# First two tiles of a fused convolution and two-layer kernel: taps on VectorE in PSUM, tap pairs on TensorE, Exp on ScalarE, narrower first weights

## The chip, the cores and the metric

One NeuronCore of a Trainium2 chip runs the kernel. The metric is the device time of one execution in microseconds (us). The five engines are TensorE (PE, matrix products), VectorE (DVE), ScalarE (ACT), GpSimd (POOL) and SyncE (SP, which here only issues transfers). Each works through its own queue in order and waits for the others at semaphores.

## What is computed

The input is x, 2 sequences of 4096 positions with 192 channels, and 8 heads of 7 taps. The taps of a head go through a softmax, each channel is convolved causally with its head's 7 taps, and two dense stages follow on the 8192 tokens:

```python
w = np.exp(weight - weight.max(-1, keepdims=True))
w = w / (w.sum(-1, keepdims=True) + 1e-09)
out = np.einsum('hk,bskhg->bshg', w, x_unf)          # 7 taps, causal
x = out.reshape(8192, 192)
x = (sigmoid(x @ w_gate) * (x @ w_val)) @ w_out       # 192 -> 1536 -> 192
h = x @ w_in                                          # 192 -> 2048
P = a[0] + a[1]*h + a[2]*h**2 + a[3]*h**3
Q = 1 + abs(b[0])*abs(h) + abs(b[1])*h**2
out = (P / (Q + 1e-6)) @ w_out2                       # 2048 -> 192
```

Weights come to the device as 64-bit floats.

## The kernel before

Channels lie on partitions: 128 in a first block, the other 64 (R) in a second. Tokens are cut into 16 tiles of 512. Every operand of a product is split into a high and a low part (fp32r), so that a 192-channel product takes five matmuls: `mm128` (lines 1027 to 1029: high weight by high x, low weight by high x, high weight by low x) and `mm64` (lines 1035 and 1036), in which the 64 channels of the second block lie twice, on the lower and the upper 64 partitions, so that high and low weights go in one matmul.

For each tile `conv` convolves, `moe1` runs pass A (gate and val, 12 blocks of 128 columns, 10 matmuls a block) and pass B (5 matmuls a block), and `moe2` runs pass C (16 blocks, 5 matmuls each) and pass D (5 matmuls each; in the last tile, 12 blocks take two full fp32 matmuls instead). That is 340 matmuls a tile.

Weights are loaded once, in pieces of columns. `to_f32` (line 794) takes a piece through a transfer, one rounding and one Prelu activation on ScalarE (lines 807 and 711) and one bit operation on VectorE (line 816); `split_rows` and `split_tail` then make the high part (a copy, mostly on ScalarE) and the low part (a subtraction, line 722). Gate and val columns come in pieces of 256, 256, 512 and 512 (`cw1`). A piece of `w_gate` rows, of `w_val` rows and of the 64 remaining rows of both must be split before the blocks of pass A which it covers can run. There are 12 buffers of kind `f` (4 KB a partition) through which raw pieces, split pieces and later values pass.

The softmax of the taps (`small`, line 739) makes exp from two sigmoids, since Sigmoid's table is needed next anyway, and normalises the taps on VectorE before anything uses them. Tile 0: the first 128 channels are convolved by VectorE, one instruction a tap, in SBUF (`conv_vector`, lines 952 and 954); the second block, for tiles 0 and 1 together, is convolved by TensorE with 7 full fp32 products against diagonal matrices of the taps (`conv_first`, line 943), which GpSimd builds (line 936). Tile 1's first block and everything from tile 2 on are convolved by GpSimd, two instructions a tap (`conv_taps`, lines 920 and 923). `warm_up` runs 18 bf16 matmuls on zeros (line 965) before.

The order of all instructions is written out by hand: `PROGRAM` lists the 4747 operations of the plan by number, with a letter where another engine than the first choice takes one; buffers of a kind are given out by a planner (`Plan.order`), which runs at build time. An operation on GpSimd that shares VectorE's port is held behind an earlier VectorE operation of that sort (the `gate` at the end of the kernel). Transfers go out from SP's queue, the four first pieces of weights from ScalarE's.

Of the kernel before, what the change touches and what calls it, by code (L numbers as in the profile page):

```python
# [90 lines left out]
class Plan:  # L91
# [50 lines left out]
    def free_slots(self, kind, sort):  # L142

        got, held = [], 0
        for i, b in enumerate(self.slots[kind]):
            if b is None:
                got.append((0.0, i))
                continue
            if b.freed is None and all(u.end is not None for u in b.users):
                b.freed = max(u.end + FREE[u.eng] for u in b.users)  # L150
            if b.freed is not None:
                got.append((b.freed, i))
            elif b.sort == sort:
                held += 1
        return [] if held >= self.caps.get(sort, 1000) else sorted(got)

    def fit(self, o):

        t, places, used = 0.0, [], set()
        for b in o.bufs:  # L160
            if b.slot is not None:
                continue
            for s, i in self.free_slots(b.kind, b.sort):
                if (b.kind, i) not in used:
                    used.add((b.kind, i))
                    places.append((b, i))
                    t = max(t, s)
                    break
            else:
                return None, None  # L170
        return t, places

    def order(self, look, switch):


        free = dict.fromkeys(ENGINES, 0.0)
        avail = {e: [] for e in ENGINES}
        table, lock_free, clock = "sig", 0.0, Clock()

        def add(o):  # L180
            for e in o.opts:
                avail[e].append(o)

        def begin(o, e):
            t = max(free[e], o.ready, lock_free if o.opts[e][2] else 0.0)
            for b in o.bufs:
                for d, end in b.last.items():
                    if d != e:
                        t = max(t, end + HOP[d][e])
            return t  # L190

        for o in self.ops:
            if o.left == 0:
                add(o)
        for _ in self.ops:
            best = None
            for eng in ENGINES:
                found = []
                for i, o in enumerate(avail[eng]):
                    start = begin(o, eng)  # L200
                    if len(o.opts) > 1:
                        ends = {e: begin(o, e) + v[0] + v[3] for e, v in o.opts.items()}
                        if ends[eng] > min(ends.values()):
                            continue
                    found.append((start, o.prio + (switch if o.table and o.table != table else 0.0), i, o,
                                  max(free[eng], o.ready)))
                found.sort(key=lambda e: e[:3])
                pick, first = None, None
                for start, prio, _, o, asked in found:
                    if first is not None and start > first + look[eng]:  # L210
                        break
                    t, places = self.fit(o)
                    if t is None:
                        continue
                    start = max(start, t)
                    if first is None or start < first:
                        first = start
                    key = (max(0.0, start - first - look[eng]), prio)
                    if pick is None or key < pick[0] or pick[1] > first + look[eng]:
                        pick = (key, start, max(asked, t), o, places, eng)  # L220
                if pick is not None and (best is None or pick[1:3] < best[0:2]):
                    best = pick[1:]
            assert best is not None, "no operation can go on"
            o, places, eng = best[2:]
            o.eng, o.start = eng, best[0]
            cost, o.emit, lock, _ = o.opts[eng]
            frees = FREES[eng] if lock is True else lock
            if o.table and table != o.table:
                cost += TABLE
                table = o.table  # L230
            if eng == "PE" and o.start > free[eng] + 1.0:
                cost += STALL / FAST
# [352 lines left out]
    warm=18,  # L585
# [30 lines left out]
def conv_gated_rational_kernel(  # L616
# [639 lines left out]
    if warm:  # L1256
        warm_up(warm)
# [65 lines left out]
```

## Time and profile before

| | |
|---|---|
| median of 3 runs (lowest to highest) | 1278.5 us (1278.0 to 1279.02) |
| the profiled execution, its own time | 1277.71 us |
| span of its trace, first to last instruction | 1275.9 us |
| mean granted TensorE clock | 0.996 |
| PE, DVE, ACT, POOL busy, share of the span | 99%, 87%, 86%, 56% |

The profile shows one execution. Busy times of an engine are of instructions in flight: a matmul of 512 columns is shown with 389 ns, while the next one starts some 227 ns after it, so a busy share of TensorE close to 100% says that matmuls follow one another, and their number in a stretch says how fast. What the engines do at the start of the kernel is read from stretches and from the list of instructions in order of time, since the page's totals are those of 16 tiles.

### The profile page before, as it was taken

To read this page: it belongs to the slowest core of one execution; us is meant where nothing else is said; L and a number is where in the kernel's file an instruction comes from. 1 tells how busy PE (TensorE), PEld (TensorE's weight loads), DVE (VectorE), ACT (ScalarE), POOL (GpSimd) and SP (SyncE) were. 2 spreads that over 40 slices of the span, in tenths; PEclk is the share of its full clock that TensorE was granted. 3 is DMA by queue.
4 is the path that set the end of the run, shared out by engine and by line. 5 is a ranking of instruction groups with operands and counts; after the bars stand their busy time and mean duration, and the time that the engine had idled before them with its cause. 6 is when DMAs were issued, how large, how long until landed. Compare 5 with 4: busy or idle time off the path is not lost.

```text
span 1275.9 us, 15239 instructions
## 1 busy us (share of the span) xinstructions
PE 1260.0 (99%) x5460; PEld 1021.4 (80%) x5460; DVE 1114.8 (87%) x1362; ACT 1094.7 (86%) x1408; POOL 708.6 (56%) x466
## 2 busy tenths in 40 slices
PE   7999999999999999999999999999999999999998
PEld 3778888888888888888888888888888888888884
DVE  6989899989889888789888988878898887889996
ACT  7988988888887989887897897889888897789996
POOL 4476656665655575763565664866454745464530
PEclk9999999999999999999999999999999999999999
DMA  7621000010000100001010010100001000000000
GB/s 200 194 79 26 1 17 13 1 38 1 5 25 1 38 1 18 13 1 38 1 29 1 9 30 1 29 1 27 12 1 29 9 22 1 1 21 1 13 13 12
DMA packets 16716, 31.01 MB, mean 24 GB/s; under 512 B 2560, under 2 KB 6272, under 8 KB 16640
## 3 DMA queue, kind: packets, MB, share of 16 engines
q1 hardware_dynamic: 16192, 29.26, 8.2%
q8 instruction: 42, 0.69, 0.2%
q10 hardware_dynamic: 448, 0.79, 0.2%
q14 instruction: 34, 0.28, 0.1%
HBM read 19.81 MB, written 6.29 MB: 20 GB/s over the span
## 4 chain that ended last, share of the span: by engine, by line
PE 92%; DVE 4%; ACT 2%; issue 1%; DMA 1%; POOL 0%; SPq 0%; DVEq 0%; ACTq 0%; POOLq 0%
PE w L1027 11%; PE w L1035 11%; PE w L1036 11%; PE w L1028 11%; PE w L1029 11%; PE accd L1052 4%; PE accd L1061 4%; PE accd L1054 4%; PE accd L1062 4%; PE accd L1053 4%; PE accb L1052 3%; PE accb L1054 3%; PE accb L1053 3%; PE accb L1061 3%; PE accb L1062 3%; ACT f L711 1%
## 5 line engine op out<-in xcount | busy, mean ns | idle before, releaser
L711 ACT ACTIVATE f<-w,av 128x512 f32<-128x512 f32 x256 | 196.2, 778 | 49.5 <-PE w L1036 45.9
L720 POOL TENSOR_TENSOR r<-f,r 128x1024 fp32r<-128x1024 f32 x66 | 178.2, 2704 | 86.9 <-DVE f L1191 13.3
L1191 DVE TENSOR_TENSOR f<-f,w 128x512 f32<-128x512 f32 x256 | 172.4, 681 | 42.7 <-ACT f L711 41.9
L711 ACT ACTIVATE f<-w,kv 128x512 f32<-128x512 f32 x256 | 171.1, 686 | 41.4 <-PE w L1036 34.0
L722 DVE TENSOR_TENSOR r<-f,r 128x1024 fp32r<-128x1024 f32 x152 | 194.3, 1285 | 9.9 <-ACT r L711 4.4
L706 POOL TENSOR_SCALAR r<-f 128x1024 fp32r<-128x1024 f32 x77 | 114.1, 1483 | 139.1 <-DVE f L1216 28.1
L1193 DVE SCALAR_TENSOR_TENSOR f<-f,av,w 128x512 f32<-128x512 f32 x256 | 186.6, 743 | 4.8 <-ACT f L711 1.0
L923 POOL TENSOR_TENSOR ca<-ca,tmp 128x512 f32<-128x512 f32 x90 | 148.6, 1652 | 68.2 <-DVE f L1216 18.5
L1216 DVE SCALAR_TENSOR_TENSOR f<-f,av,f 128x1024 f32<-128x1024 f32 x128 | 171.7, 1347 | 9.4 <-ACT f L711 9.3
L1197 DVE SCALAR_TENSOR_TENSOR f<-f,bv 128x1024 f32<-128x1024 f32 x128 | 168.1, 1319 | 10.4 <-ACT f L711 10.2
L711 ACT ACT_TABLE_LOAD x130 | 166.8, 1283 | 5.0 <-DVE f L1197 1.5
L1097 DVE TENSOR_TENSOR f<-f,w 128x512 f32<-128x512 f32 x192 | 130.4, 681 | 46.2 <-PE w L1036 26.6
L920 POOL TENSOR_SCALAR tmp<-xa,cw 128x512 f32<-128x512 f32 x90 | 103.5, 1150 | 107.2 <-DVE f L1216 25.6
L711 ACT ACTIVATE f<-f,kv 128x1024 f32<-128x1024 f32 x128 | 156.4, 1241 | 1.2 <-DVE f L1197 0.3
L711 ACT ACTIVATE f<-f 128x1024 f32<-128x1024 f32 (+3 forms) x160 | 151.8, 960 | 0.8 <-DVE wo_s L870 0.2
L711 ACT ACTIVATE f<-w 128x512 f32<-128x512 f32 x192 | 113.2, 594 | 35.7 <-PE w L1036 32.6
L711 ACT ACTIVATE r<-f 128x1024 fp32r<-128x1024 f32 x99 | 103.8, 1056 | 10.4 <-DVE f L1097 4.7
L1027 PE MATMUL w<-yha,w_h 128*128 128x512 f32 x256 | 100.1, 391 | 0.2
L1029 PE MATMUL w<-yla,w_h 128*128 128x512 f32 x256 | 99.7, 389 | 0.0
L1028 PE MATMUL w<-yha,w_l 128*128 128x512 f32 x256 | 99.7, 389 | 0.0
L1036 PE MATMUL w<-ylb,w_b 128*128 128x512 f32 x256 | 99.6, 389 | 0.0
L1035 PE MATMUL w<-yhb,w_b 128*128 128x512 f32 x256 | 99.6, 389 | 0.0
(152 smaller groups left out, 3095.7 us busy)
## 6 DMA issues: line engine op xcount, KB each, us to landing
f<-in_wo SPq DMA_DIRECT2D x14, 384.0 KB, 3.7
xa<-in_xt SPq DMA_DIRECT2D x16, 259.0 KB, 3.2
out_dram<-f SPq DMA_DIRECT2D x16, 256.0 KB, 2.6
xb<-in_xt SPq DMA_DIRECT2D x16, 129.5 KB, 2.9
f<-in_w SPq DMA_DIRECT2D x4, 512.0 KB, 4.3
out_dram<-f SPq DMA_DIRECT2D x16, 128.0 KB, 2.4
xhb<-xhb SPq DMA_DIRECT2D x15, 128.0 KB, 2.3
xlb<-xlb SPq DMA_DIRECT2D x15, 128.0 KB, 2.2
```

Of the source, the lines that this page charges most:

```text
L711: plan.op("ACT", (53 if psum else 95) + n * 0.832 + 93 * ptr + own, prio, lambda: nc.scalar.activation(out=out(), in_=in_(), func=func, ** ...
L720: alts.append(("POOL", 147 + n * 2.105, lambda: nc.gpsimd.tensor_tensor(out=out(), in0=in0(), in1=f(in1()), op=ALU.subtract), True, H[alt] ...
L722: dve(prio, n, lambda: nc.vector.tensor_tensor(out=out(), in0=in0(), in1=f(in1()), op=ALU.subtract), rd, wr, lock=lock, alts=alts)
L1027: nc.tensor.matmul(o, lhsT=wh.tile[:, c], rhs=ha, start=True, stop=False)
L1028: nc.tensor.matmul(o, lhsT=wl.tile[:, c], rhs=ha, start=False, stop=False)
L1029: nc.tensor.matmul(o, lhsT=wh.tile[:, c], rhs=la, start=False, stop=False)
L1035: nc.tensor.matmul(o, lhsT=wb.tile[:, c], rhs=hb, start=False, stop=False)
L1036: nc.tensor.matmul(o, lhsT=wb.tile[:, c], rhs=lb, start=False, stop=True)
L1191: dve(at("v", t, p), sn, lambda q=q, cut=cut, h=h: nc.vector.tensor_tensor(out=cut(u[q]), in0=cut(u[q]), in1=h(), op=ALU.mult), [ps_, (u[q ...
L1193: dve(at("w", t, p), sn, lambda q=q, cut=cut, h=h: nc.vector.scalar_tensor_tensor(out=cut(u[q]), in0=cut(u[q]), scalar=av.tile[:, 1:2], in ...
L1197: dve(at("y", t, p), gn, lambda q=q: nc.vector.scalar_tensor_tensor(out=C(ha[q]), in0=C(ha[q]), scalar=bv.tile[:, 0:1], in1=C(ha[q]), op0= ...
L1216: dve(at("g", t, p), gn, lambda k=k: nc.vector.scalar_tensor_tensor(out=C(u[k]), in0=C(u[k]), scalar=av.tile[:, 0:1], in1=C(ha[k]), op0=AL ...
```

## The change

The order text is another one (4777 operations), and a second text, `SLOTS`, gives each buffer its place; the planner's `order`, `fit`, `free_slots` and `Clock` go. In it:

- `small` takes exp with ScalarE's Exp, then at once a Sigmoid on one element. Taps are used unnormalised (`cwe`); the sum and its reciprocal are made beside, and the reciprocal comes in as the scale of the operations that split the convolved tile (`xs`). The normalised taps for the later tiles are one GpSimd operation.
- For tiles 0 and 1 VectorE convolves the first block, now with the running sum in PSUM (`conv_vector`; bank `accd1`). TensorE convolves the second block with two taps per product: the 64 channels lie twice on the partitions, the second copy one token later (`load_pair`), and 4 products a tile take taps 0 and 1, 2 and 3, 4 and 5, and 6 (`pair_weights`, `conv_pairs`). Their output has both copies that `mm64` wants. Tile 1 is so no longer convolved on GpSimd.
- The first weights are 128, 128, 256, 512 and 512 columns wide; all of them come over SP's queue, and ScalarE's queue loads `xa` of tile 0.
- 12 matmuls on zeros instead of 18; their zeros are written by VectorE.
- Which engine takes a copy or a subtraction is now the order text's choice alone. Of the 218 copies that make high parts of `moe1` and `moe2` values it puts 99 on ScalarE, 75 on GpSimd and 44 on VectorE; of the 20 low parts of gate and val weights 12 on GpSimd and 8 on VectorE.

```diff
-        plan.op("DVE", 350, START, sm, rd=[cw], wr=[cw, wsum])
-        def ex():
-            nc.scalar.activation(out=ng, in_=w, func=ACTF.Sigmoid, scale=-1.0)
-            nc.scalar.activation(out=w, in_=w, func=ACTF.Sigmoid)
...
+        plan.op("DVE", 400, START, sm, rd=[cw, z], wr=[cw, wsum])
+        plan.op("ACT", 230, START, lambda: nc.scalar.activation(out=cwe.tile, in_=w, func=ACTF.Exp), rd=[cw], wr=[cwe])
+        plan.op("ACT", 200 + 1283, START, lambda: nc.scalar.activation(
+            out=first.tile, in_=cwe.tile[:, 0, 0:1], func=ACTF.Sigmoid), rd=[cwe], wr=[first])
+        for r0, k0, m in ((0, 0, 4), (R, 1, 3)):
...
+            plan.op("ACT", 200, START + 1, pick_act, rd=[cwe], wr=[(cwp, r0)],
+                    alts=[("POOL", 200, pick_pool, True, H["dg"]["POOL"])])
+        plan.op("DVE", 180, START + 12, lambda: nc.vector.tensor_reduce(
+            out=t(1), in_=cwe.tile, axis=mybir.AxisListType.X, op=ALU.add), rd=[cwe], wr=[wsum])
...
+        plan.op("POOL", 250, START + 13, lambda: nc.gpsimd.tensor_tensor(
+            out=w, in0=cwe.tile, in1=over(3), op=ALU.mult), rd=[cwe, wsum], wr=[cw], lock=True)
...
-            queue = (lambda k: None if i else 0.1 * k)
+            queue = (lambda k: None)
...
+    def pair_weights(eye):
+        plan.op("POOL", 147 + 2.105 * R, START, lambda: nc.gpsimd.tensor_tensor(
+            out=T(eye)[:, 128:128 + R], in0=T(eye)[:, 0:R], in1=T(eye)[:, R:2 * R], op=ALU.add),
+            rd=[(eye, "i")], wr=[(eye, "e")], lock=True)
+        got = []
+        for j in range(4):
+            d = Buf("f", "dg")
+            m = R if j == 3 else 2 * R
...
+            plan.op("ACT", 95 + 128 * 0.832 + 93, START + 2 + j, lambda diag=diag, ones=ones, sc=sc: nc.scalar.activation(
+                out=diag(), in_=ones(), func=ACTF.Copy, scale=sc()), rd=[(eye, "e"), cwp], wr=[d],
...
+    def load_pair(t, x):
+        n = tiles[t][1]
+        def both():
+            nc.sync.dma_start(out=T(x)[0:R, 0:n + HALO], in_=tile_src(t, 128, D))
+            nc.sync.dma_start(out=T(x)[R:2 * R, 0:n + HALO - 1], in_=tile_src(t, 128, D)[:, 1:n + HALO])
+        dma(START + 1 + 50 * t, 512 * (n + HALO), both, [x], k=2)
+    def conv_pairs(n, x, pairs_, prio, o):
+        for j, (d, m) in enumerate(pairs_):
+            plan.op("PE", pe32(n), prio, lambda d=d, j=j, m=m: nc.tensor.matmul(
+                T(o)[:, 0:n], lhsT=T(d)[0:m, 0:128], rhs=T(x)[0:m, 2 * j:2 * j + n], start=(j == 0), stop=(j == 3)),
+                rd=[x, d, o] if j else [x, d], wr=[o])
+        return o
...
+    def conv_vector(t, n, x, i, acc):
+        def y():
+            return T(acc)[:, 0:n]
+        plan.op("DVE", 131 + 1.04 * n, START + 60 * t, lambda: nc.vector.tensor_scalar(
+            y(), T(x)[:, 0:n], cwe.tile[:, i, 0:1], 0.0, op0=ALU.mult, op1=ALU.add), rd=[x, cwe], wr=[acc], lock=False)
+        for k in range(1, TAPS):
+            plan.op("DVE", 150 + 1.04 * n, START + 60 * t + k, lambda k=k: nc.vector.scalar_tensor_tensor(
+                out=y(), in0=T(x)[:, k:k + n], scalar=cwe.tile[:, i, k:k + 1], in1=y(), op0=ALU.mult, op1=ALU.add),
+                rd=[x, cwe, acc], wr=[acc], lock=False)
...
+        if t < 2:
+            xa, ca = Buf("xa"), Buf("accd1")
+            xb, cb = (Buf("f", "xb1"), Buf("accd2")) if t else (Buf("xb"), hot)
...
+                plan.op("ACT", 480.0, START - 1, lambda: nc.scalar.dma_start(
+                    out=T(xa)[:, 0:n + HALO], in_=tile_src(t, 0, 128)), wr=[xa])
...
+            for hi, lo, src, i in ((xha, xla, ca, 0), (xhb, xlb, cb, 1)):
+                act(at("xs", t, q + i), n, lambda hi=hi: T(hi)[:, 0:n], lambda src=src: T(src)[:, 0:n], [src, wsum], [hi],
+                    func=ACTF.Copy, psum=True, scale=wsum.tile[:, i, 3:4])
...
-    warm=18,
+    warm=12,
-    cw1=[256, 256, 512, 512],
+    cw1=[128, 128, 256, 512, 512],
```

The start of the new order, engine by engine, in words (`0g`, `0v`, `0b` are the gate rows, the val rows and the 64 remaining rows of both in the first piece, `1g` those of the second, and so on):

- SP: taps, identity, 0v, 0g, `xb` of tile 0 (two transfers), `xb` of tile 1 (two), 1g, 0b (two), 1v, 1b (two), 2g, 2b (two), b, `xa` of tile 1, 2v, 3g, 3b, the first `w_out` piece, 3v. ScalarE issues `xa` of tile 0 first of all.
- ScalarE: Exp, a pick of taps, round and Prelu of 0v and of 0g, the one-element Sigmoid, round 1g, the third diagonal, round 0b, Prelu 1g, Prelu 0b, the fourth diagonal, round 1v, `xha`, Prelu 1v, Prelu 1b, round 2g, `xhb`, round 2b, Prelu 2g, Prelu 2b, and copies of the `b` parts.
- VectorE: zeros, maximum and difference, sum, tap 0, a small one, tap 1, bits of 0v, bits of 0g, taps 2 and 3, reciprocal, taps 4 and 5, low part of 0g, bits of 1g, tap 6, low part of 1g, round 1b, bits of 0b, `xla`, three operations on pieces, `xlb`, bits of 2g and 2b, then the taps of tile 1 one at a time between pieces and `gv` products.
- TensorE: 12 matmuls on zeros, then first pair of tile 0, first of tile 1, second and third of tile 0, second of tile 1, fourth of tile 0, third of tile 1, then pass A: `mm128` of gate block 1, gate 0 and val 0, `mm64` of gate 0 and 1, and so on through both blocks, the fourth pair of tile 1, blocks 2 and 3, and then the blocks of the 512-wide pieces.

## Rows read from the trace of the kernel before

**Rows 1.** The page's first part: busy time, share of the span and instructions.
```profile
PE 1260.0 (99%) x5460; PEld 1021.4 (80%) x5460; DVE 1114.8 (87%) x1362; ACT 1094.7 (86%) x1408; POOL 708.6 (56%) x466
```
**Rows 2.** Stretches: from:to, length, busy us (instructions) per engine, clock, DMA share, GB/s.
```profile
0.00:16.00 16.00, 12.33 (x34) 4.88 (x34) 8.64 (x21) 8.55 (x20) 2.66 (x7) 1.00 0.67 190
5.00:10.00 5.00, 3.02 (x11) 1.27 (x10) 2.03 (x8) 2.27 (x7) 1.94 (x2) 1.00 1.06 261
15.30:64.80 49.50, 43.31 (x170) 32.79 (x170) 43.42 (x75) 46.69 (x88) 26.41 (x21) 0.93 0.67 196
28.00:30.00 2.00, 0.92 (x2) 0.82 (x3) 0.69 (x4) 2.00 (x5) 1.65 (x2) 0.50 0.59 150
200.00:400.00 200.00, 200.00 (x883) 165.25 (x882) 177.28 (x207) 170.00 (x214) 120.97 (x77) 1.00 0.05 13
```
**Rows 3.** TensorE's waits: line and releaser, total us, times, longest.
```profile
PE w L1027 <- ACT f L711: 4.6, 2, 3.8
...
PE accb L1052 <- ACT r L711: 1.4, 1, 1.4
```
**Rows 4.** TensorE in order of time: start, us, line, count, [idle before, releaser].
```profile
1.31 5.36 PE L965 MATMUL w<-zeros 128*128 128x512 bf16 x18 [1.31 <-POOL zeros L961]
...
8.65 6.25 PE L943 MATMUL w<-xb,f 128*128 128x512 f32 x14 [1.98 <-DMA xb<-in_xt]
...
15.27 0.50 PE L1027 MATMUL w<-xha,wg_h 128*128 128x512 f32 x1 [0.37 <-ACT xha L711]
...
29.09 0.79 PE L1027 MATMUL w<-xha,wg_h 128*128 128x512 f32 x1 [3.76 <-ACT f L711]
29.68 0.63 PE L1028 MATMUL w<-xha,wg_l 128*128 128x512 f32 x1
30.10 0.63 PE L1029 MATMUL w<-xla,wg_h 128*128 128x512 f32 x1
...
64.52 0.39 PE L1062 MATMUL accb<-r,wo_s 128*128 128x512 f32 x1
```
**Rows 5.** VectorE in order of time, same columns, the first 17 us.
```profile
3.67 0.17 DVE L751 TENSOR_TENSOR cw<-cw,wsum 128x14 f32<-128x14 f32 x1
...
9.35 0.49 DVE L952 TENSOR_SCALAR ca<-xa,cw 128x512 f32<-128x512 f32 x1 [0.19 <-DMA xa<-in_xt]
9.87 4.69 DVE L954 SCALAR_TENSOR_TENSOR ca<-xa,cw,ca 128x512 f32<-128x512 f32 x6
...
16.08 0.68 DVE L722 TENSOR_TENSOR xla<-ca,xha 128x512 fp32r<-128x512 f32 x1
```
**Rows 6.** ScalarE in order of time, same columns, at the start and near the end.
```profile
2.86 1.28 ACT L756 ACT_TABLE_LOAD   x1 [2.86 <-issue]
...
14.59 0.63 ACT L711 ACTIVATE xha<-ca 128x512 fp32r<-128x512 f32 x1 [1.46 <-DVE ca L954]
...
1260.04 1.28 ACT L711 ACT_TABLE_LOAD   x1
...
1261.33 1.06 ACT L711 ACTIVATE f<-f 128x1024 f32<-128x1024 f32 x1
```
**Rows 7.** Transfers: two issues on SP's queue, two landings in the chain, one wait.
```profile
0.73 0.39 SPq L740 DMA_DIRECT2D cw<-in_wt  x1
2.11 2.41 SPq L989 DMA_DIRECT2D xb<-in_xt  x2
...
0.74 3.30 DMA f<-in_wg
4.57 4.68 DMA xa<-in_xt
...
SPq L989 <- DMA f<-in_wg: 1.3, 1, 1.3
```
**Rows 8.** The page's groups: shapes, count, busy us, mean ns, idle before.
```profile
L706 POOL TENSOR_SCALAR r<-f 128x1024 fp32r<-128x1024 f32 x77 | 114.1, 1483 | 139.1 <-DVE f L1216 28.1
L1193 DVE SCALAR_TENSOR_TENSOR f<-f,av,w 128x512 f32<-128x512 f32 x256 | 186.6, 743 | 4.8 <-ACT f L711 1.0
```

More of the change, by code (lines that the diff above doesn't have):

```diff
@@ L140, in op @@
         self.ops.append(o)
[L142 to L185, printed above, removed]
-            for b in o.bufs:
[L187 to L232, printed above, removed]
-            o.end = clock.run(o.start, cost) if eng == "PE" else o.start + cost
-            for b in o.bufs:
-                if b.bank:
-                    b.last[eng] = o.end
-            for e in o.opts:
-                avail[e].remove(o)
-            free[eng] = o.end + (POOLGAP if eng == "POOL" else 0.0)
-            if lock:
-                lock_free = max(o.start, o.end - frees)
-            for b, i in places:
-                b.slot = i
-                self.slots[b.kind][i] = b
-            for d in o.out:
-                d.left -= 1
-                d.ready = max(d.ready, o.end + (TAIL[eng] if d.eng == eng else HOP[eng].get(d.eng or "ACT", 0.0)))
-                if d.left == 0:
-                    add(d)
-        self.length = max(o.end + FREE[o.eng] for o in self.ops)
-        return sorted(self.ops, key=lambda o: o.start)
@@ L253, in program @@
-    def program(self, text):
+    def program(self, text, slots):
+        places = iter("".join(slots.split()))
+        for o in self.ops:
+            o.eng, (_, o.emit, *_) = next(iter(o.opts.items()))
+            for b in o.bufs:
+                if b.slot is None:
+                    b.slot = int(next(places), 36)
         order = []
@@ L767, in small, with pick, pick_act, pick_pool @@
-        plan.op("DVE", 1300, START, nm, rd=[cw, wneg], wr=[cw, wsum, wneg])
+        plan.op("DVE", 400, START, sm, rd=[cw, z], wr=[cw, wsum])
[3 more added lines that the diff above has]
+        for r0, k0, m in ((0, 0, 4), (R, 1, 3)):
+            def pick(e, r0=r0, k0=k0, m=m):
+                return cwp.tile[r0:r0 + R, 0:m], cwe.tile[r0:r0 + R, 1, k0:TAPS:2]
+            def pick_act(pick=pick):
+                o, i = pick(0)
+                return nc.scalar.activation(out=o, in_=i, func=ACTF.Copy)
+            def pick_pool(pick=pick):
+                o, i = pick(0)
+                return nc.gpsimd.tensor_scalar(o, i, 1.0, 0.0, op0=ALU.mult, op1=ALU.add)
+            plan.op("ACT", 200, START + 1, pick_act, rd=[cwe], wr=[(cwp, r0)],
+                    alts=[("POOL", 200, pick_pool, True, H["dg"]["POOL"])])
@@ L1019, in conv @@
-        rows[t] = (xha, xla, xhb, xlb)
+        act(at("xs", t, q + 1), n, lambda: T(xhb)[h:h + R, 0:n], lambda: T(cb)[h:h + R, 0:n], [cb], [(xhb, h)], alt="xy")
+        minus(at("xs", t, q + 1), n, lambda: T(xlb)[h:h + R, 0:n], lambda: T(cb)[h:h + R, 0:n],
+              lambda: T(xhb)[h:h + R, 0:n], [cb, (xhb, h)], [(xlb, h)])
+        for b in (xhb, xlb):
+            dma(at("xd", t, q), 256 * n, lambda b=b: nc.sync.dma_start(
+                out=f(T(b)[R - h:2 * R - h, 0:n]), in_=f(T(b)[h:h + R, 0:n])), [(b, R - h)], rd=[(b, h)])
```

577 lines of the change are left out of this document (281 added, 296 removed), and 109 rows, old and new, of tables (PROGRAM, off).

## The prediction

> **What bounds the kernel now.** I read the shares first [rows 1], then a table of stretches [rows 2], TensorE's waits [rows 3], and the first 65 us in order of time [rows 4 to 7]. TensorE is busy 99% of the span. In the steady state it starts 883 products in 200 us [rows 2], one per 0.2265 us, with VectorE and ScalarE at 85 to 89%: there only fewer products or a shorter one would help, and the change touches neither. What is left is the start. The first product of pass A begins at 15.27 us and the 170th at 64.52 [rows 4], so its slot ends at 64.75. 170 products at 0.2265 us are 38.5 us; the stretch has 49.5 [rows 2]: 11.0 us are lost in it, beside the 15.27 ahead of it. The losses are seen in order of time: the product at 29.09 comes after a wait of 3.76 us for ScalarE, the clock is then 0.50, the lower of the two levels (1.2 GHz), and products start 0.42 apart [rows 2 to 4]. What TensorE waits for there are weights that ScalarE and VectorE are splitting.
>
> The chain to 15.27: `xa` is issued at 4.57 and lands 4.68 us later [rows 7]; VectorE takes its first tap at 9.35 and six more in 4.69 us, ending at 14.56 [rows 5]; ScalarE makes `xha` at 14.59 [rows 6], VectorE `xla` at 16.08 [rows 5]. TensorE's own seven products end at 14.9 [rows 4], off this chain.
>
> **The change, step by step.**
>
> *The tile lands earlier.* `xa` goes out first on ScalarE's queue. The transfer first there now, of 262 KB against `xa`'s 265, was issued at 0.74 and landed at 4.05 [rows 7]. So VectorE is no longer waiting for data but for Exp: the difference ends at 3.84 [rows 5], the table is loaded by then (today a load takes from 2.86 to 4.14 behind four issues [rows 6]; now there is one issue ahead of it), Exp takes some 0.25, the sum 0.2: tap 0 at 4.5.
>
> *The taps.* A dependent tap now starts every 0.785 us (4.69 for six, [rows 5]). With the sum in PSUM no row shows one; the nearest reads PSUM and writes SBUF, 0.743 [rows 8]. I take 0.785, bounds 0.68 (the `xla` row [rows 5]) to 0.9. Seven taps are 5.5 us; among them stand eight small operations on taps and 128-column pieces, some 0.17 to 0.25 us each, 1.3 together: the taps end near 11.2. `xha` then ends at 11.9 (0.63, [rows 6]) and `xla` at 12.6. One wait stands in this queue: the bits of 1g stand ahead of the last tap, and they wait for ScalarE, which has round 0b ahead of Prelu 1g. SP's queue waits for an earlier landing once many transfers are out (its second `xb` issue waited 1.3 us for the first landing [rows 7]); with 0b issued near 5.2 and 5.7 and 3.3 to 4.7 us to land [rows 7] it is there by 8.5 to 10.4, Prelu 1g by 9.1 to 11.0. The last tap is due at 10.4: between 0 and 0.9 us, I take 0.
>
> *TensorE's taps.* 12 matmuls on zeros end near 5.2: 18 took 5.36 [rows 4], without the last six, at 0.227 each, 4.0, and they start at about 1.2 as now. The first diagonal is ready near 6.0 (tap pick, then one GpSimd operation), `xb` between 5.5 and 6.5. Seven fp32 products stand ahead of pass A; seven took 6.25 [rows 4]: 6.1 + 6.2 + 0.3 for diagonals made by ScalarE = 12.6. That ends level with `xla`. The idle stretch before them, 1 us, is shorter than the 1.98 us after which today's ran at a clock of 1.00 [rows 2, 4], so I price no fall. **First product: 12.7 instead of 15.27, -2.6 us.**
>
> The added table load runs on ScalarE from about 5.9 to 7.2, under the taps. Here the trace has 1260.04 for a load of 1.28 and 1261.33 for the next activation [rows 6]: 1.29 in all. The Trainium skill (ScalarE: Activation LUTs, What ACT_TABLE_LOAD costs) says 1.28 and a drain of 1.38 behind it, 2.66 for each change of table. By the page Prelu 1g and the third diagonal would be 1.4 later, the first product 0.3 to 0.5 later and the time near 1270.5; no drain is in these rows, and I go by them.
>
> *The ramp to the 170th product.* 170 products are 38.5 us, and the fourth pair of tile 1, which stands among them, 0.9. With pieces of 128 columns the first two blocks can be fed from 12.7 on: I followed 1g, 0b, 2g and 2v through the queues, with the 0.63 and 0.68 of the `xha` and `xla` rows [rows 5, 6] scaled to their columns, and they arrive within some tenths of their use, to 22.6 us. Then the 512-wide piece 3g is needed: it can be issued only when VectorE has freed its buffer (12.9), lands near 17.6, and passes round, Prelu, bits, copy and low part behind the `sig`, `gv` and tap work, ready at 23.5 to 23.9: a wait of 1.3, instead of 3.76 and the slow clock. Beyond that I bound by VectorE. It was busy 8.6 us in the first 16 and 43.4 in the stretch [rows 2], 51 us by 64.8, so idle for more than 13. The change adds tile 1's seven taps, 5.5, and takes away about as much: five or more low parts that go to GpSimd (2.1), normalisation and narrow pieces (1.2), and operations that now stand behind this point (2.5). So again 51 us, started at 3.5: not before 54.5, and with 2 us of waits 56.5. By TensorE: 12.7 + 38.5 + 0.9 + 1.3 = 53.4, and 3 us for waits of VectorE's pace give the same 56.4. The low bound is 53.4; the high one, with 5 of today's 13 us of VectorE's idle time, 59.5. **Lost in the stretch after the change 5.2 instead of 11.0, -5.8 us.**
>
> *Behind it.* A wait of 1.4 us at the first `hi1` of the last pair follows today [rows 3]; I leave it, bounds -1.5 and +3. The steady state: the order text keeps TensorE's sequence from its 300th to its 1300th entry of 1557, and its 218 high copies are spread 99, 75 and 44 over ScalarE, GpSimd and VectorE; GpSimd has 77 today [rows 8]. So 0, bounds -1 and +2. The last two tiles are ordered a little differently, the products at the end are the same: 0.
>
> **Sum.** -2.6 - 5.8 = -8.4. On the profiled execution's own time of 1277.71 that is 1269.3; the median lies 0.8 above that execution, which gives 1270.1. I say 1270.
>
> **Rivals.**
> 1. *VectorE stays starved in the ramp.* The waits are not removed but moved: two tiles' taps and the splitting share one queue, and an operation that waits for ScalarE or a transfer holds all behind it. For it: VectorE idled 13 us of 64.8 today; late 0b or 3g would hold taps. With 59.5 to 61.5 at the 170th product the gain is 3.3 to 5.3: 1273 to 1275. The rule that speaks for it is in the Trainium skill (DMA: Bandwidth & Descriptors, Bandwidth): small transfers move less per us, 64 KB in 0.95 us and 1 MB in 6.15. From that I estimate some 1.8 us more for the first 0.8 MB in six pieces of 128 KB than in three of 256; rows here show only that 7 KB took about as long to land (the difference started at 3.67 after an issue at 0.73 [rows 5, 7]) as 262 KB, 3.3.
> 2. *The clock falls.* If a landing leaves TensorE idle as long as today's 3.76 before its fp32 products, or before 3g, the rows at 28 us come back: 0.42 instead of 0.23 a product [rows 2, 4]. On the seven fp32 products that is 6 us, with some 10 products more, 8 us: no gain, 1278. Against it: the longest idle stretch that I find is 1.3.
> 3. *Slower: taps in PSUM.* 12 of the 14 taps read and write one bank, which no row shows. Each 0.1 us more costs 1.4 us on the queue that bounds the ramp. From 0.6 more, 1.4 us a tap, the gain is gone; at twice today's 0.785 it costs 11 us: 1281. For it: nothing but that it isn't shown. Against: the row that reads PSUM is no slower than the one that doesn't [rows 5, 8].
> 4. *Better.* All of it arrives in time and the later wait goes too: 53.4 and -1.5: 1265.5.
>
> **Chances and range.** Forecast (1267 to 1272.5) 0.56, rival 1 0.22, rival 2 with others that return the gain 0.08, rival 3 and other losses 0.07, rival 4 0.07. The range from 1264.5 to 1276 leaves out rivals 2 and 3 and a little of 4. About 0.2%, 2.6 us, is what a measurement of this kernel can tell from no change. Faster by more than that: 0.56 + 0.22 + 0.07 = 0.85; within it 0.08; slower 0.07.
>
> **What would show it.** Tap 0 near 4.5 and a tap every 0.8 us; `xha` between 11.2 and 12; TensorE's fp32 products without a hole from about 6.1, clock 1.00; the first product of pass A at 12.7; TensorE's longest wait below 2 us and near 23; the 170th product near 56; VectorE busy 51 us by then with few idle us; after 100 us some 441 products per 100 us as now. The prediction is wrong if the last tap waits behind the bits of 1g, if the clock shows 0.50 anywhere in the first 30 us, or if the steady rate changes.

## The result and the profile after

The changed kernel takes 1265.6 us (median of 4 runs, 1265.48 to 1266.15) beside 1278.25 us (4 runs, 1277.97 to 1279.02) for the kernel before: a ratio of 0.9901, 95% interval 0.9884 to 0.9918. That is 12.65 us less; 8.5 were forecast (1270.0), and the range, 1264.5 to 1276.0, holds the time. The profiled execution took 1265.66 us, its span 1263.6.

The page's shares (of the changed kernel, as the next fences to the experiments) answer [rows 1]:

```profile
PE 1257.4 (100%) x5456; PEld 1020.2 (81%) x5456; DVE 1108.8 (88%) x1376; ACT 1091.2 (86%) x1405; POOL 698.4 (55%) x469
```

The totals hardly move. The stretches show more; columns as in [rows 2]:

```profile
0.00:16.00 16.00, 14.74 (x38) 6.40 (x39) 11.56 (x29) 11.14 (x30) 4.96 (x19) 1.00 0.69 202
5.00:10.00 5.00, 4.92 (x12) 1.77 (x11) 4.26 (x11) 3.53 (x10) 1.59 (x5) 1.00 0.66 179
12.90:52.60 39.70, 39.67 (x166) 30.35 (x165) 38.01 (x70) 39.26 (x77) 14.50 (x17) 1.00 0.83 232
200.00:400.00 200.00, 200.00 (x883) 165.07 (x882) 175.36 (x207) 169.34 (x211) 119.99 (x76) 1.00 0.05 13
```

In the first 16 us VectorE is busy 11.56 us instead of 8.64, and ScalarE 11.14 instead of 8.55. From the first product to 52.6 us TensorE has no hole to speak of, the granted clock is 1.00, and the steady state has the 883 products in 200 us that it had before.

TensorE's waits in the whole execution, all that are listed, answer [rows 3]; the second stands at 67.83, behind the 170th product:

```profile
PE w L832 <- DVE zeros L828: 1.2, 1, 1.2
PE w L900 <- ACT f L541: 0.2, 1, 0.2
```

TensorE in order of time, beside [rows 4] (L809 is a two-tap product, L900 and L901 are `mm128`, and 54.20 is the 170th product):

```profile
1.19 5.30 PE L832 MATMUL w<-zeros 128*128 128x512 bf16 x12 [1.19 <-DVE zeros L828]
6.42 1.20 PE L809 MATMUL w<-xb,f 128*128 128x512 f32 x2
...
12.38 1.13 PE L809 MATMUL accd<-f,f 128*128 128x512 f32 x2
12.94 0.79 PE L900 MATMUL w<-xha,wg_h 128*128 128x512 f32 x1
...
18.01 1.12 PE L809 MATMUL accd<-f,f 64*128 64x512 f32 x2
...
23.75 0.43 PE L900 MATMUL w<-xha,wg_h 128*128 128x512 f32 x1
24.19 0.50 PE L901 MATMUL w<-xha,wg_l 128*128 128x512 f32 x1
...
54.20 0.39 PE L935 MATMUL accb<-r,wo_s 128*128 128x512 f32 x1
```

So the first product of pass A comes 2.33 us earlier (15.27 to 12.94), the 170th 10.32 earlier (64.52 to 54.20), and the span is 12.3 shorter: 2.3 are won ahead of the first product, 8.0 between it and the 170th, 2.0 behind it.

VectorE and ScalarE, beside [rows 5, 6]:

```profile
3.85 0.74 DVE L818 TENSOR_SCALAR accd<-xa,cwe 128x512 f32<-128x512 f32 x1
...
9.77 0.29 DVE L661 SCALAR_TENSOR_TENSOR f<-f,f 128x128 int32<-128x128 int32 x1 [0.29 <-ACT f L541]
9.98 0.75 DVE L821 SCALAR_TENSOR_TENSOR accd<-xa,cwe,accd 128x512 f32<-128x512 f32 x1
...
11.48 0.75 DVE L864 SCALAR_TENSOR_TENSOR xla<-accd,wsum,xha 128x512 fp32r<-128x512 f32 x1 [0.22 <-ACT xha L541]
```

```profile
5.94 1.28 ACT L588 ACT_TABLE_LOAD   x1
7.24 0.20 ACT L588 ACTIVATE first<-cwe 128x1 f32<-128x1 f32 x1
...
10.76 0.69 ACT L541 ACTIVATE xha<-accd,wsum 128x512 fp32r<-128x512 f32 x1
...
18.71 0.68 ACT L652 ACTIVATE f<-f 128x512 int32<-128x512 uint32 x1
```

The chain to the first product is now TensorE's own. `xla` ends at 12.23, and the seventh two-tap product at 12.9. The chain of waits goes back over these products to the landing of tile 1's rows of the second block:

```profile
4.47 3.18 DMA f<-in_xt
...
7.69 1.12 PE accd L809 x2
```

### The profile page after: what moved, and what is told of

Read it like the earlier page. It is cut to its first block, busy times and chain, and to the rows that moved or that the text cites. A ratio compares the mean times of both kernels' runs of the same rounds, so it can differ in the third digit from the quotient of the medians.

```text
span 1263.6 us, 15268 instructions
## 1 busy us (share of the span) xinstructions
PE 1257.4 (100%) x5456; PEld 1020.2 (81%) x5456; DVE 1108.8 (88%) x1376; ACT 1091.2 (86%) x1405; POOL 698.4 (55%) x469
## 4 chain that ended last, share of the span: by engine, by line
PE 97%; ACT 2%; SPq 0%; DMA 0%; issue 0%; DVE 0%; ACTq 0%
PE w L900 11%; PE w L901 11%; PE w L902 11%; PE w L908 11%; PE w L909 11%; PE accd L935 4%; PE accd L927 4%; PE accd L926 4%; PE accd L925 4%; PE accd L934 4%; PE accb L934 3%; PE accb L935 3%; PE accb L927 3%; PE accb L926 3%; PE accb L925 3%; PE accd L931 1%
## 5 line engine op out<-in xcount | busy, mean ns | idle before, releaser
L550 POOL TENSOR_TENSOR r<-f,r 128x1024 fp32r<-128x1024 f32 x64 | 174.3, 2728 | 83.3 <-ACT r L541 11.3
L536 POOL TENSOR_SCALAR r<-f 128x1024 fp32r<-128x1024 f32 x75 | 110.4, 1474 | 134.7 <-DVE f L1089 21.7
L769 POOL TENSOR_TENSOR ca<-ca,tmp 128x512 f32<-128x512 f32 x84 | 139.6, 1662 | 69.1 <-DVE f L1089 18.5
L541 ACT ACTIVATE f<-f 128x1024 f32<-128x1024 f32 (+4 forms) x163 | 152.0, 945 | 0.5
L900 PE MATMUL w<-yha,w_h 128*128 128x512 f32 x256 | 99.9, 390 | 0.0
L901 PE MATMUL w<-yha,w_l 128*128 128x512 f32 x256 | 99.6, 389 | 0.0
```

Of the source, the lines that this page charges most:

```text
L541: plan.op("ACT", (53 if psum else 95) + n * 0.832 + 93 * ptr + own, prio, lambda: nc.scalar.activation(out=out(), in_=in_(), func=func, ** ...
L550: alts.append(("POOL", 147 + n * 2.105, lambda: nc.gpsimd.tensor_tensor(out=out(), in0=in0(), in1=f(in1()), op=ALU.subtract), True, H[alt] ...
L900: nc.tensor.matmul(o, lhsT=wh.tile[:, c], rhs=ha, start=True, stop=False)
L901: nc.tensor.matmul(o, lhsT=wl.tile[:, c], rhs=ha, start=False, stop=False)
```

## Experiments

| run | median us (lowest to highest) | ratio to before, 95% interval |
|---|---|---|
| `after_again`: the changed kernel, unaltered | 1265.66 (1265.52 to 1267.18) | 0.9905 (0.9890 to 0.9920) |
| xa_late | 1267.55 (1267.21 to 1269.74) | 0.9920 (0.9904 to 0.9937) |
| wide_pieces | 1267.82 (1266.76 to 1269.50) | 0.9920 (0.9905 to 0.9934) |
| taps_sbuf | 1266.78 (1266.57 to 1266.97) | 0.9910 (0.9895 to 0.9925) |
| two_sigmoids | 1266.64 (1265.76 to 1267.29) | 0.9909 (0.9894 to 0.9923) |
| one_tap | 1265.89 (1265.73 to 1266.15) | 0.9905 (0.9890 to 0.9919) |
| warm1 | 1266.84 (1266.48 to 1269.11) | 0.9918 (0.9901 to 0.9934) |
| tuned | 1267.06 (1266.43 to 1268.87) | 0.9915 (0.9901 to 0.9928) |
| before_taps_first | 1281.11 (1279.94 to 1282.62) | 1.0023 (1.0013 to 1.0032) |
| before_xa_first | 1279.24 (1278.81 to 1281.92) | 1.0009 (1.0000 to 1.0018) |
| sig_early | 1279.24 (1278.32 to 1280.13) | 1.0004 (0.9995 to 1.0013) |
| scalar_relief | 1279.16 (1278.23 to 1280.63) | 1.0005 (0.9996 to 1.0015) |

The first eight are the changed kernel, or it with one thing altered (`tuned` alters several); the last four are the kernel before with one thing altered. Single runs of one kernel spread by 0.4 to 3.1 us, so differences of tenths between medians say little. Numbers in the diffs are operations of the order text.

**xa_late.**

```diff
-                plan.op("ACT", 480.0, START - 1, lambda: nc.scalar.dma_start(
+                plan.op("SP", 480.0, START - 1, lambda: nc.sync.dma_start(
-0 2 247 1 249 248 31 16 255 3
+0 2 1 249 31 16 255 247 248 3
```

> The changed kernel with one step undone: tile 0 goes out on SP's queue behind the two issues of xb (as before the change), where a transfer now leaves at 3.83 us, instead of first on ScalarE's queue. It should land near 7.1 us instead of 3.6, so tap 0 moves from 3.85 to about 7.1 (+3.3). Some 0.9 us of VectorE's idle time ahead of xla goes, so xla ends near 14.9 instead of 12.2 and the first product of pass A comes at 15.0 instead of 12.94, +2.1. Theory 1 (TensorE has next to no idle time behind its first product, so what is lost at the start is lost at the end): 1267.5 to 1268.5. Theory 2 (the ramp absorbs it, because VectorE's pace and not TensorE's sets the 170th product): 1265.5 to 1266.3. Theory 3 (the 2 us that TensorE then idles lower its clock): 0.50 in the rows behind 13 us and 1270 or more.

VectorE's first tap and TensorE in `xa_late`:

```profile
7.00 0.75 DVE L818 TENSOR_SCALAR accd<-xa,cwe 128x512 f32<-128x512 f32 x1 [3.82 <-DMA xa<-in_xt]
```

```profile
8.57 1.12 PE L809 MATMUL accd<-f,f 128*128 128x512 f32 x2 [1.38 <-DMA f<-in_xt]
...
14.48 0.79 PE L900 MATMUL w<-xha,wg_h 128*128 128x512 f32 x1
```

The first product comes 1.54 us later, and the time is 1.95 longer: theory 1. What is lost ahead of the first product is lost at the end, since TensorE has no idle time later in which to win it back; the 0.4 beyond it is about the size of a wait for a sigmoid at 25.92 (0.41), where the changed kernel lost 0.2 at 24.19. The tap is 3.15 us late; `xla`, which had 0.7 us to spare, ends 2.3 late, at 14.55; TensorE's two-tap products, held at 8.57 by tile 1's rows, which now land behind `xa`, end at 14.48. The two chains tie again.

**wide_pieces.**

```diff
-    cw1=[128, 128, 256, 512, 512],
+    cw1=[256, 256, 512, 512],
```

> The changed kernel with the first two pieces of 128 columns of the first weights joined to one of 256 (as before the change), the transfers at the first piece's places, the rest of the work at the second piece's. Theory 1 (the narrow pieces are what feeds the first products, as the prediction had it): products of the first block wait for 256 columns where they waited for 128; TensorE waits 0.5 to 2 us between 13 and 20 us, the time is 1266.2 to 1267.7. Theory 2 (the narrow pieces only cost instructions: twelve of 0.2 us fewer on VectorE and ScalarE before 13 us, some 0.3 to 0.6 us off the path to xla): first product 12.9, no new wait, 1265.0 to 1265.8.

The order text shrinks with it to 4756 operations, and the text of the buffers' places to match. TensorE in `wide_pieces`:

```profile
7.65 1.10 PE L808 MATMUL w<-xb,f 128*128 128x512 f32 x2 [1.19 <-DMA xb<-in_xt]
...
16.76 0.50 PE L907 MATMUL w<-xhb,wg_b 128*128 128x512 f32 x1 [0.36 <-POOL wg_b L549]
```

The median is 0.1 above theory 1's range, as two runs took 1266.8 and two 1268.9 and 1269.5; the profile is of one at 1266.8, 1.1 longer than the changed kernel, and what the others lost more isn't shown. In it only 0.36 us is the wait that theory 1 named. The larger part is ahead of the first product: `xb`, issued at the same times behind two pieces twice as large, lets the first two-tap product start at 7.65 instead of 6.42, and the first of pass A comes at 13.75, 0.81 later. In this execution the narrow pieces work above all by what they leave free for other transfers.

**taps_sbuf.**

```diff
-            xa, ca = Buf("xa"), Buf("accd1")
+            xa, ca = Buf("xa"), Buf("ca")
```

> The changed kernel with the sums of VectorE's taps for tiles 0 and 1 in SBUF instead of PSUM, nothing else moved. Theory 1 (a tap that reads and writes PSUM costs what one in SBUF does: a tap started each 0.785 us before in SBUF, 0.79 after in PSUM): taps 0.74 to 0.80 us each, time within 0.3 us of 1265.6. Theory 2 (PSUM makes them dearer or spares them a wait for the port that VectorE shares with GpSimd): seven taps differ by 0.5 us or more, first product by as much, time by 0.3 to 1.5 us.

GpSimd building the first diagonal and copying the first high part, in the changed kernel:

```profile
4.45 0.38 POOL L793 TENSOR_SCALAR f<-f,cwp 128x128 f32<-128x128 f32 x1
...
6.33 0.30 POOL L536 TENSOR_SCALAR wg_h<-f 128x128 fp32r<-128x128 f32 x1 [1.50 <-DVE f L661]
```

and in `taps_sbuf`:

```profile
4.51 0.88 POOL L793 TENSOR_SCALAR f<-f,cwp 128x128 f32<-128x128 f32 x1
...
6.45 0.74 POOL L536 TENSOR_SCALAR wg_h<-f 128x128 fp32r<-128x128 f32 x1 [1.07 <-DVE f L661]
```

The first product is no later (12.83). The loss of 1.2 us comes behind it: GpSimd's operations beside VectorE's taps take about twice as long, and GpSimd is busy 8.43 us of the first 16 instead of 4.96. The first 512-column piece slips with them: its transfer is issued at 12.90 instead of 12.46, and its rounding on ScalarE, which waits 0.87 for the landing, starts at 19.67 instead of 18.71. The time is in theory 2's range, but not by its mechanism: VectorE's taps of tile 0 take 0.74 to 0.77 us as before (only the first, with one input, is shorter: 0.48 instead of 0.74), and the first product doesn't move. For these six later taps the sum in PSUM isn't dearer for VectorE, and it is cheaper for GpSimd.

**two_sigmoids.**

```diff
-        plan.op("ACT", 230, START, lambda: nc.scalar.activation(out=cwe.tile, in_=w, func=ACTF.Exp), ...
+            nc.scalar.activation(out=wneg.tile, in_=w, func=ACTF.Sigmoid, scale=-1.0)
+            nc.scalar.activation(out=cwe.tile, in_=w, func=ACTF.Sigmoid)
+            nc.vector.reciprocal(wneg.tile, wneg.tile)
+            nc.vector.tensor_tensor(out=cwe.tile, in0=cwe.tile, in1=wneg.tile, op=ALU.mult)
```

> The changed kernel with the exponential undone: two sigmoids on ScalarE, reciprocal and product on VectorE, as before the change, so one table load in place of two. Tap 0 moves from 3.85 to about 4.5 (one activation and two small VectorE operations of 0.17 to 0.2 us, and a hop), the load of 1.28 us at 5.94 goes. Theory 1 (TensorE's warm-up and its seven fp32 products, ending at 12.9, and the taps, ending in xla at 12.2, tie; a delay of 0.6 us on the taps' side is nearly hidden): first product 12.9 to 13.1, time 1265.4 to 1266.0. Theory 2 (the load on ScalarE holds up round, Prelu and diagonals that TensorE waits for): 0.3 to 1 us faster. Theory 3 (the taps are the only chain to the first product): 0.6 us slower, 1266.2.

Tap 0 starts at 4.69 and the first product at 12.92, as theory 1 says. Two of the four runs took 1265.8 and 1266.0, two 1267.3; the profile is of one of the latter, and shows a collision. VectorE and GpSimd in `two_sigmoids`:

```profile
24.61 1.70 DVE L667 SCALAR_TENSOR_TENSOR f<-f,f 128x384 int32<-128x384 int32 x1
```

```profile
24.60 1.29 POOL L550 TENSOR_TENSOR wg_b<-f,wg_b 64x512 fp32r<-64x512 f32 x1 [4.03 <-DVE wg_b L539]
```

The same bit operation takes 0.54 us in the changed kernel, where it starts at 24.39 and GpSimd's subtraction, starting at 24.55, takes 1.55. In these rows whichever starts first goes through, and the other ends only after it. Here GpSimd was first by 0.01 us, and TensorE waited 0.9 for the gate-by-value product queued behind. In the profiled run the loss is thus a collision; by the two faster runs the exponential and the table load are worth nothing that can be told from no change.

**one_tap.**

```diff
-            ... START + 60 * t + k, lambda k=k: nc.vector.scalar_tensor_tensor(
+            ... START + 60 * t + k, lambda k=k: None if t else nc.vector.scalar_tensor_tensor(
```

> The changed kernel without the last six of VectorE's seven taps of tile 1 (left out of the computation: tile 1's upper 128 channels are then convolved by the first tap alone), 4.7 us less on VectorE between 15.5 and 32 us. Theory 1 (VectorE's queue paces the ramp to the 170th product, as the prediction had it): the wait at 23.75 goes and 1 to 2 us come back, 1263.6 to 1264.7. Theory 2 (what is left of the loss is TensorE's own, or comes from the landing of the 512-column piece at 18.7 us): 1265.2 to 1265.8.

The ramp of `one_tap`, and its collision:

```profile
12.90:52.60 39.70, 39.05 (x164) 29.87 (x163) 35.38 (x63) 38.65 (x76) 13.48 (x17) 1.00 0.80 228
```

```profile
24.13 1.52 DVE L661 SCALAR_TENSOR_TENSOR f<-f,f 128x384 int32<-128x384 int32 x1 [0.27 <-ACT f L541]
```

VectorE has 2.6 us less to do in the stretch, and the time is the same within 0.3 us, 0.1 above theory 2's. Being early even hurt a little: the bits come behind GpSimd's subtraction (23.94 to 25.23), and TensorE waits 0.65 at 26.30. The 170th product comes at 54.84; without those 0.65 it would come where the changed kernel has it (54.20), not 1 to 2 us earlier. So VectorE's amount of work doesn't set the changed kernel's ramp.

**warm1.**

```diff
-    warm=12,
+    warm=1,
```

> The changed kernel with 1 matmul on zeros instead of 12: TensorE stands nearly idle from 1.7 to about 6.2 us, when xb lands. Theory 1 (the warm-up buys the clock for the fp32 products): granted clock 0.50 and fp32 products at twice today's 0.88 us each for some or all of the seven, first product of pass A at 15 to 19 us, time 1267.5 to 1272. Theory 2 (the products find the higher clock without it): they start at 6.2 instead of 6.42 and the rest is unchanged, 1265.2 to 1265.8.

TensorE in `warm1`:

```profile
6.40 2.05 PE L809 MATMUL w<-xb,f 128*128 128x512 f32 x2 [4.61 <-DMA xb<-in_xt]
8.24 1.81 PE L809 MATMUL accd<-f,f 128*128 128x512 f32 x2
9.88 1.88 PE L809 MATMUL w<-xb,f 128*128 128x512 f32 x4
```

The first two of the seven products start 1.84 and 1.64 us after one another, the rest 0.86. The first product of pass A comes 1.22 later (14.16) and the time is 1.2 longer: the slow products of theory 1, at less than its price, as only two are slow. The matmuls on zeros are worth that. That the clock is the cause isn't shown: the column of the granted clock has 1.00 for the stretch, where theory 1 had 0.50.

**before_taps_first**, an early tile and early taps alone:

```diff
-10 0 2 27 223 ... 5 12a 13 224 29 ... 36 226 7
+224 10 0 2 27 223 ... 5 226 12a 13 29 ... 36 7
```

> The kernel before with one step of the change alone: tile 0 goes out first on ScalarE's queue (the first weights' transfers there each leave some 0.5 us later), and VectorE's seven taps stand ahead of the bits of the first pieces. The taps then run from about 5.8 to 11.2 us instead of 9.35 to 14.56, in time that VectorE idled. TensorE's own seven products still end near 14.9, so the first product of pass A comes at 14.9 instead of 15.27 at best. Theory 1 (the wait of 3.76 us at 29 us and the low clock behind it come from VectorE's backlog, which is 3 us shorter now): the wait shrinks to 1 to 2 us, no 0.50 in the clock, 1271.5 to 1275.5. Theory 2 (what is waited for at 29 us is set by the landing of the weights and by ScalarE): the wait stays at 3 to 4 us, 1277.5 to 1278.7.

GpSimd's diagonals and TensorE in `before_taps_first`:

```profile
7.16 1.12 POOL L935 TENSOR_TENSOR f<-f,cw 128x384 f32<-128x384 f32 x1 [5.90 <-DVE cw L765]
13.17 1.16 POOL L935 TENSOR_TENSOR f<-f,cw 128x512 f32<-128x512 f32 x1 [4.89 <-DVE f L815]
```

```profile
10.28 2.81 PE L942 MATMUL w<-xb,f 128*128 128x512 f32 x6 [2.94 <-DMA xb<-in_xt]
14.39 1.99 PE L942 MATMUL w<-xb,f 128*128 128x512 f32 x4 [1.29 <-POOL f L935]
...
33.37 0.79 PE L1026 MATMUL w<-xha,wg_h 128*128 128x512 f32 x1 [3.75 <-ACT f L710]
```

It is 2.9 us slower, which neither theory had. With `xa` ahead of it `xb` lands 1.6 later, and GpSimd makes the second group of diagonals only behind the bits that now follow VectorE's taps, where the kernel's own `gate` holds it (both groups were done at 7.77 before); the first product comes at 17.52. The wait that followed is as long as before (3.75). The transfers were full: the DMA share from 5 to 10 us was 1.06 before the change [rows 2], is 0.96 in this run, and 0.66 after the change.

**before_xa_first**, the early tile with VectorE's order left as it was:

```diff
-10 0 2 27 223 ... 13 224 29
+224 10 0 2 27 223 ... 13 29
```

> The kernel before with tile 0 sent out first on ScalarE's queue and VectorE's order left as it was, so that the bits of the second piece, which wait for its landing near 8.7 us, still stand ahead of the taps. Theory 1 (the early landing alone is worth nothing, since VectorE's first tap started at 9.35 anyway, 0.2 us behind those bits): first tap 9.2 to 9.8, 1278 to 1279.5. Theory 2 (it brings part of what the whole change brought at the start): first tap before 8, first product 0.5 us or more earlier, 1277.5 or less.

VectorE in `before_xa_first`:

```profile
10.13 0.43 DVE L815 SCALAR_TENSOR_TENSOR f<-f,f 128x256 int32<-128x256 int32 x1 [2.89 <-ACT f L710]
10.47 0.48 DVE L951 TENSOR_SCALAR ca<-xa,cw 128x512 f32<-128x512 f32 x1
```

The tap waits behind those bits and is 1.1 us later than before, 0.7 beyond what theory 1 allowed; the median is within theory 1. The profiled run is one of the slower (1280.58): in it `xb` lets TensorE's own products start at 9.74 instead of 8.65, and the first product of pass A comes at 17.12 instead of 15.27. So in that execution the early tile alone costs at the start.

**sig_early.**

```diff
-257 74 274 251 ... 9 260 63 262
+257 260 74 274 251 ... 9 63 262
```

> The kernel before with one instruction moved: the sigmoid of the gate sums that ScalarE starts at 28.45 us, behind seven steps of the weights' splitting, stands directly behind the two products that complete these sums (ended near 24.5). The product at 29.09 writes the bank of PSUM that this sigmoid reads. Theory 1 (TensorE's wait of 3.76 us is for that bank, so for ScalarE's queue, and not for weights; the low clock follows from the wait): the wait is below 0.8 us, no 0.50 behind it, and of the 3.8 us and some 2.2 us of slow products most comes back: 1272.5 to 1275. Theory 2 (the weights of these products are what is late, as the prediction read it): the wait stays above 2.5 us, 1277 to 1278.5.

TensorE in `sig_early`, and the waits that answer [rows 3]:

```profile
26.99 0.40 PE L1028 MATMUL w<-xla,wg_h 128*128 128x512 f32 x1
33.06 0.79 PE L1034 MATMUL w<-xhb,wg_b 128*128 128x512 f32 x1 [5.68 <-DVE wg_b L721]
```

The wait of 3.76 us for the bank is gone, six products run at once, and then TensorE waits 5.68 for the low part of the first 512-column piece; the product on it starts at 33.06 instead of 32.16, and the clock of 0.50 comes behind this wait instead (32 to 36 us). Both theories hold a part, the releaser was the bank, and the weights stood behind it; the time is 0.7 above what either gave.

**scalar_relief**, three copies moved from ScalarE to VectorE:

```diff
-257 74 274 251 50 46 51 ... 52 53 84
+257 74v 274 251 50 46v 51 ... 52 53v 84
```

> The kernel before with three copies of high parts (0.62, 0.42 and 0.40 us on ScalarE between 24.2 and 27.4 us) made by VectorE instead, at the same places of the order, where VectorE waits; ScalarE is busy 16.66 of the 17.00 us from 16 to 33. Theory 1 (ScalarE's queue paces the splitting, so the bank and the weights that TensorE waits for at 29.09 and 32.16 come 1.4 us earlier): the wait at 29.09 is 2.2 to 2.6 us instead of 3.76, time 1276.2 to 1277.2. Theory 2 (VectorE's queue paces it, as the prediction had it): 1.2 us more of its work, the wait is 3.7 us or more, 1278 to 1279.5.

ScalarE and TensorE in `scalar_relief`:

```profile
27.08 0.43 ACT L710 ACTIVATE f<-f 128x256 f32<-128x256 f32 x1 [1.56 <-DVE wv_b L708]
```

```profile
30.27 0.50 PE L1026 MATMUL w<-xha,wg_h 128*128 128x512 f32 x1 [4.01 <-ACT f L710]
```

ScalarE's time is saved and lost again at once: its next Prelu writes a buffer that one of the moved copies still reads, and that copy stands on VectorE behind a low part of 1.21 us. Theory 2's time, but its reason isn't shown: the wait that grew is one of ScalarE for VectorE. Together with `sig_early` this speaks for two queues that hand the pace to and fro, neither setting it alone.

**tuned.**

```diff
-    warm=12,
+    warm=10,
-560 36p 10 ... 11 264 261 253 ... 41p 561 13
+36p 10 ... 11 264 560 561 261 253 ... 41p 13
-298 88 122 292 293 84 296 ... 299 124 294
+298 84 88 293 122 292 296 ... 299 294 124
```

> The changed kernel with 10 matmuls on zeros instead of 12, TensorE's two-tap products in an order in which the third diagonal isn't needed until tile 1's first two have freed its buffer (both of tile 0's first, then both of tile 1's), and near 23 us one sigmoid ahead of one rounding on ScalarE, the low part of the 512-column piece ahead of other bits and one product of gate and value ahead of the bits of the output weights on VectorE. Theory 1 (TensorE's chain sets the first product, and what is lost at 23.75 to 25.6 us is the order of these queues): first product 12.3 instead of 12.94, 0.3 to 0.5 less lost at 23.75, 1264.4 to 1264.9. Theory 2 (other waits take their place): 1265.3 to 1266.

TensorE in `tuned`:

```profile
6.50 1.96 PE L809 MATMUL w<-xb,f 128*128 128x512 f32 x4 [1.06 <-DMA xb<-in_xt]
...
12.65 0.79 PE L900 MATMUL w<-xha,wg_h 128*128 128x512 f32 x1
...
25.51 0.50 PE L900 MATMUL w<-xha,wg_h 128*128 128x512 f32 x1 [0.80 <-ACT f L541]
```

Two matmuls on zeros fewer win nothing, since `xb` lands at 6.5. The new pair order wins 0.3 us at the first product, and a sigmoid that now comes later (24.88 instead of 24.02) takes 0.80: other waits take their place, as theory 2 says, though the time is 1.1 above its range. No run beat the changed kernel.

## Why the prediction was right, and where not

**The tile lands earlier, the taps: right.** Tap 0 was forecast at 4.5 and started at 3.85 (the difference of the taps, from which Exp starts, ended 0.36 us earlier than in the kernel before). A tap in PSUM takes 0.74 to 0.76 us, and one that follows another starts some 0.79 after it, where 0.785 was taken and 0.68 to 0.9 bounded. `xla` ends at 12.23 (12.6). The wait for the bits of 1g, given between 0 and 0.9, was 0.29. The prediction named a last tap that waits behind these bits as a sign of being wrong; it did wait, by 0.29, and it cost nothing, as `xla` had 0.7 to spare. Rival 3 asked for 1.4 us a tap; `taps_sbuf` turns it round, since the sums in SBUF cost 1.2 us more in all.

**TensorE's taps: right.** The tie with `xla` was called, to 0.7 us, and 12.7 measured 12.94. The sum had `xb` there by 6.1 and the matmuls on zeros done at 5.2, taking the six saved ones at 0.227 each. In the profiled execution all 12 ran at some 0.44, to 6.4, and the two-tap products stand right behind them. But this is not what set the start, as the same kernel in `after_again` shows:

```profile
1.19 4.27 PE L832 MATMUL w<-zeros 128*128 128x512 bf16 x12 [1.19 <-DVE zeros L828]
6.55 1.10 PE L809 MATMUL w<-xb,f 128*128 128x512 f32 x2 [1.09 <-DMA xb<-in_xt]
```

There the 12 take 4.27, TensorE waits for `xb`, and the first product comes at 12.99. The 0.24 comes from the transfers: `xb` lands at 6.3 to 6.5 where 6.1 was taken (5.5 to 6.5 were given), and tile 1's rows, for the second of these products, at 7.65.

**The table load: right.** The next activation started 1.30 us after the load did. No drain of 1.38 stands behind it, which the Trainium skill (ScalarE: Activation LUTs, What ACT_TABLE_LOAD costs) asks for: the measurement decides, and a kernel without that load wasn't faster.

**The ramp to the 170th product: the mis-sized term.** Forecast was a loss of 5.2 us, after 11.0. Measured: 170 products from 12.94 would end the last slot at 51.44, and it ends at 54.43, a loss of 3.0, of which 1.1 is the fourth pair of tile 1 at 18.01 (17.70 to 19.07 between the products around it, beyond one slot; forecast 0.9). This term gave 8.0 us instead of 5.8. Two steps in it failed.

- The wait at the first 512-column piece was put at 1.3 us near 22.6; it is 0.2 at 24.19 (0.44 us after the product at 23.75). The piece landed only at 18.7, not 17.6, so ScalarE's rounding starts at 18.71; but TensorE needs it 1.1 us later than forecast, and the path behind it had no further wait.
- The bound "by VectorE" (51 us of its work, 2 to 3 us of waits) isn't what limits. Up to the 170th product VectorE is busy 48.57 us in 54.4, and `one_tap` shows that 2.6 us less of it change nothing.

These rows of the changed kernel and of the kernel before, from the start to the 170th product, say where the 10.3 us went:

```profile
0.00:54.40 54.40, 53.11 (x198) 35.88 (x199) 48.57 (x97) 49.21 (x101) 19.29 (x33) 1.00 0.79 225
```

```profile
0.00:64.80 64.80, 54.94 (x202) 37.40 (x202) 51.36 (x94) 54.54 (x106) 29.07 (x28) 0.95 0.67 195
...
16.00:33.00 17.00, 11.24 (x38) 7.71 (x38) 13.48 (x27) 16.66 (x35) 10.77 (x9) 0.85 0.72 202
```

ScalarE has 5.3 us less work by then and idles 5.2 instead of 10.3; VectorE has 2.8 less and idles 5.8 instead of 13.4. The prediction weighed VectorE's idle time alone. In the kernel before ScalarE was busy 16.66 of the 17 us in which TensorE waited most. GpSimd has 9.8 less (19.29 beside 29.07); tile 1 is no longer convolved there. Which of these differences lets the ramp run without holes is argued from these rows; no run takes one away alone.

**The reading of the wait at 29.09: half right.** "Weights that ScalarE and VectorE are splitting" are what TensorE lacks, but the wait in [rows 3] ends with a bank of PSUM that a sigmoid frees, queued on ScalarE behind the splitting. `sig_early` moves that sigmoid, and the wait moves on to the weights.

**Behind it: off by 2.** Forecast 0; it is -2.0. The wait of 1.4 for `hi1` [rows 3] is gone from the list of waits; the other 0.6 isn't traced. The prediction had the loss of that wait as the low bound and in rival 4, whose 1265.5 is the time that came, though by a 170th product at 54.20 and not at 53.4. Why that wait went wasn't tried. So the range held, but the measured time lies below the band of the forecast (1267 to 1272.5), in the case that was given a chance of 0.07.

**The other rivals.** Rival 1 (VectorE starved) asked for the 170th product at 59.5 or later and fell with 54.20. Its estimate from the Trainium skill (DMA: Bandwidth & Descriptors, Bandwidth), 1.8 us more for small pieces, finds no support here: with the pieces joined `xb` lets TensorE start 1.2 later, and the time is 1.1 longer in the profiled run, 2.2 in the median. Rival 2 (the clock) didn't happen; `warm1` prices 11 of the 12 matmuls on zeros at 1.2 us.

**What stays open.** Undoing single parts returns 2.0 (`xa_late`), 1.1 to 2.2 (`wide_pieces`), 1.2 (`taps_sbuf`) and 0 to 1.0 (`two_sigmoids`). That is 4.3 to 6.4 of the 12.65 us, a third to a half, if they added up, which wasn't tried (`warm1` undoes no part of the change, as the kernel before has 18 matmuls on zeros). The two-tap products, tile 1 off GpSimd and the new order as a whole weren't tried alone. The four single moves in the kernel before gave nothing or cost up to 2.9.

## What to carry over

This start, which several engines share, was won by moving its parts together: with the transfers full and two queues handing work to and fro, one early operation alone only moved the wait. Before pricing a wait by the work of one engine, follow what its end releases and what the next instruction needs as well, a bank and then the weights behind it. Once the ramp has no hole, a microsecond lost ahead of the first product is about a microsecond lost at the end (1.54 became 1.95, 1.22 became 1.2), while tenths won there can be lost again to a collision or a later sigmoid. And look at a second execution before explaining tenths.

## What was not expected of the hardware

- VectorE's bit operation on 384 columns took 0.54, 1.52 or 1.70 us, by whether it started 0.16 us ahead of GpSimd's subtraction, 0.19 behind it or 0.01 behind it. The Trainium skill (SBUF — State Buffer, SBUF: two separate sides) says that the port pair which the two share is locked for a whole instruction by whichever starts first, and the rows agree. Beside taps that keep their sum in PSUM GpSimd's scalings of 128x128 took 0.30 to 0.38 us, beside taps in SBUF 0.73 to 0.89.
- The 12 matmuls on zeros took 5.30 us in one execution of the changed kernel, 0.44 each, about twice the 0.2265 of the steady state, and 4.27 in another (`after_again`), so that some ran at the faster pace. The 18 of the kernel before took 5.36, and 6.68 in `sig_early`, which doesn't touch them. The column of the granted clock shows 1.00 for all these stretches.
